# Optional expert tiles moved to the front of a routed MoE stage, behind one condition

## The chip, the core and the metric

One core of a Trainium2 chip runs the whole program. The metric is device time in microseconds; lower is better. Five engines work side by side, each with an instruction queue of its own: TensorE (PE in the profile, its weight loads PEld), VectorE (DVE), ScalarE (ACT), GpSimd (POOL) and SyncE (SP, which issues most DMAs). They meet only through semaphores. A condition at run time is evaluated by each engine that has instructions in its body: it loads a value into a register (TENSOR_LOAD), compares and branches.

## The reference

```python
x = retention(q, k, v)                 # 8 x 8 heads x 576 x 64, becomes x[4608, 512]
logits = x @ w_gate + modality_bias[modality_id]       # 8 experts
e_idx = argmax(logits); gate_w = softmax(logits)[e_idx]
for e in range(8):                     # first mixture: each token goes to one expert
    out[e_idx == e] = gate_w * (relu(x[e_idx == e] @ w1[e]) @ w2[e])
# second, soft mixture over out: 32 slots
logits = out @ phi
d = softmax(logits, over tokens); slot_input = d.T @ out
slot_out = relu(slot_input @ m1[e]) @ m2[e]            # 4 slots for each of 8 experts
y = softmax(logits, over slots) @ slot_out
```

## The kernel before

**Three stages.** First the retention over 36 chunks of 128 tokens (written to `xd`), with the gate and a routing that scatters each token's number and gate weight to its expert's place in a table `tb`. Then the expert slots. Last the soft mixture's two layers and the output (lines 614 to 690).

**The slots.** Sorted by expert, the tokens fill tiles of 128; an expert's last tile is partly empty. There are at most NSLOT = 43 tiles and at least NSURE = 36; how many there are, `tot`, is known only at run time. `slot(i)` (line 530 on) works on tile i: 24 matmuls of 512 columns (L473, numbered m = 1 to 24; the first 12 give half h=0 of the hidden layer, the others h=1), each weight split into a high part `wh` and a low part `wl`. Between them stand hooks: `at(n, f)` puts f behind matmul n. So the parts of three tiles overlap in one slot: `emit_xT` for the next tile, `emit_hT`, `emit_l2` for the one before, the softmax parts `emit_sel`, `emit_z`, `emit_G` for the one before that. `places(i+4)` (SyncE) loads a tile's rows of `tb`, `gather(i+3)` (GpSimd) fetches the tokens by them.

**Change of expert.** `if_change(k, engines, f)` runs f on the engines named if tile k belongs to another expert than tile k-1. At a change the new expert's w1, waiting in `raw[h]`, is split into `wh[h]` and `wl[h]`, in four pieces each: ScalarE copies (L106), VectorE subtracts pieces 0 and 1 (L111), GpSimd pieces 2 and 3 (L107). The hooks for this are s0 = 17 (h=0) and s1 = 24 (h=1), with VectorE's share under conditions of its own at d0 = 17 and d1 = 25, which is m = 1 of the next slot. Behind it `load_raw` loads the next expert's half, and one slot later `emit_SI` adds up what the old expert's tokens give (L518 to L527).

**Index chain.** A table R on partition 0, one row for each slot and one ahead of them (`reg(-1, ...)`), holds the row numbers and flags that the conditions and loads read (lines 357 to 391).

**Start of the slots** (from line 574): `places(0..3)`; then GpSimd gathers tiles 0 and 1, `emit_xT(0)`, and GpSimd issues the loads of the first needed w1 halves and w2; the conditions for splitting w1 anew; `early` under a condition (it isn't taken here).

**End of the slots.** Slots 0 to 35 stand in one straight line. From 36 on `more(i)` nests: if n > i, slot i and `more(i+1)`, else `drain(i-1)`, which finishes the last two tiles and multiplies the result into `siT` (L604). So there are eight copies of `drain`, one for each possible end. The weights of the stage behind are loaded into memory that comes free (`piece`, `load_XL`, `later`); in the slots from 35 on these loads carry a condition, so that only the last slot's are carried out. L631 is the first product that reads `siT`.

Of the kernel before, what the change touches and what calls it, by code (L numbers as in the profile page):

```python
# [6 lines left out]
ET=mybir.EngineType  # L7
# [16 lines left out]
def host(inp):  # L24
# [40 lines left out]
    cm[6:8,368]=np.arange(2)+6  # L65
# [14 lines left out]
P=dict(A=3,B=10,wc=13,SI=14,s0=17,s1=24,d0=17,d1=25)  # L80
def body(nc,tc,I,O):
# [8 lines left out]
    with ctx, tc.manual_schedule():  # L90
# [252 lines left out]
        t8=U("t8",[E,E]); nxt=U("nxt",[E,1]); ic=U("ic",[E,NSLOT]); b1=U("b1",[E,NSLOT]); r4x=U("r4",[E,4*NSLOT+1]); r4=r4x[:,:4*NSLOT].rearrange("p (a b) -> p a b",a=4); ef=U("ef",[128,NSLOT+1]); sb=U("sb",[128,NSLOT]); rem=T("rem",[128,NSLOT])  # L343
        R=T("R",[1,NSLOT+1,4],I32); ec=U("ec",[1,NSLOT]); same=T("same",[128,NSLOT]); es=ef[:,1:]; o_=slice(0,1); i8=it[0:E]
# [9 lines left out]
        def mm_r4():  # L354
# [17 lines left out]
            lambda: V.tensor_scalar(out=r4[:,1],in0=b1,scalar1=beg,scalar2=None,op0=ALU.mult),
            lambda: V.tensor_scalar(out=r4[:,2],in0=b1,scalar1=cnt,scalar2=None,op0=ALU.mult),
            lambda: V.tensor_scalar(out=r4[:,3],in0=b1,scalar1=nxt,scalar2=None,op0=ALU.mult),
# [15 lines left out]
            lambda: V.scalar_tensor_tensor(out=rem,in0=sb,scalar=-128.0,in1=cp[3][:,2],op0=ALU.mult,op1=ALU.add)],  # L390
# [7 lines left out]
        Gs=M1.tile([128,257],F32,name="Gs"); V.memset(Gs,0.0)  # L398
# [29 lines left out]
        for t in xg: V.memset(t,0.0)  # L428
        for t in hh: V.memset(t[:,:,256],1.0)
# [10 lines left out]
        for j in range(6):  # L440
            ring("ui",j,6,[128,1],U32,pl=P0)
# [90 lines left out]
        def slot(i,first=False):  # L532
# [6 lines left out]
            if i+1<NSLOT: at(P['wc'],lambda: emit_wc(i+1))  # L539
            if NSURE<=i+2<=NSLOT: at(P['wc'],lambda: SP.dma_start(out=XW,in_=half(NPF+3,1),cond=nsp==i+2))  # L540
# [162 lines left out]
```

## Time and profile before

| | us |
|---|---|
| median of 3 runs | 651.0 (650.69 to 653.0) |
| profiled execution | 651.03 |
| its span in the profile | 649.4 |
| TensorE busy | 598.3 |
| VectorE / ScalarE / GpSimd busy | 319.1 / 208.5 / 245.9 |
| mean granted TensorE clock | 0.967 of full speed |

The retention takes the span up to about 178 us, the slots from 188 to 559, the rest is the end. [...] In a row of the order in time the bracket at the end tells how long the engine had been idle and what ended that; "issue" means that the profile shows nothing that it waited for, and a name with q (ACTq L530) is an engine's queue at a condition of that line.

### The profile page before, as it was taken

To read this page: it belongs to the slowest core of one execution; us is meant where nothing else is said; L and a number is where in the kernel's file an instruction comes from. 1 tells how busy PE (TensorE), PEld (TensorE's weight loads), DVE (VectorE), ACT (ScalarE), POOL (GpSimd) and SP (SyncE) were. 2 spreads that over 40 slices of the span, in tenths; PEclk is the share of its full clock that TensorE was granted. 3 is DMA by queue.
4 is the path that set the end of the run, shared out by engine and by line. 5 is a ranking of instruction groups with operands and counts; after the bars stand their busy time and mean duration, and the time that the engine had idled before them with its cause. 6 is when DMAs were issued, how large, how long until landed. Compare 5 with 4: busy or idle time off the path is not lost. (4 is left out here: it accounts for less than half of the span.)

```text
span 649.4 us, 17574 instructions
## 1 busy us (share of the span) xinstructions
PE 598.3 (92%) x6122; PEld 441.1 (68%) x6122; DVE 319.1 (49%) x934; ACT 208.5 (32%) x545; POOL 245.9 (38%) x351
## 2 busy tenths in 40 slices
PE   8899999999989999988999999999998999779982
PEld 5788888888557667755677777777775777453552
DVE  2455555667616443575455444545555544322342
ACT  1222323343225232453233233233343232212242
POOL 3534445545646233374343344344355343110000
PEclk8999999999979999988999999999999999889997
DMA  8999999997958820147455554444414401849888
GB/s 301 405 369 389 415 417 395 372 340 256 360 212 301 327 85 5 38 148 280 163 167 167 167 164 140 136 147 154 167 28 158 166 11 40 313 168 360 340 290 292
DMA packets 48247, 148.58 MB, mean 229 GB/s; under 512 B 12276, under 2 KB 23935, under 8 KB 37888
## 3 DMA queue, kind: packets, MB, share of 16 engines
q1 hardware_dynamic: 41936, 132.60, 55.8%
q0 software_dynamic: 6192, 14.53, 6.5%
q8 instruction: 58, 0.95, 0.6%
q14 instruction: 61, 0.50, 0.2%
HBM read 291.93 MB, written 27.71 MB: 492 GB/s over the span
## 5 line engine op out<-in xcount | busy, mean ns | idle before, releaser
L473 PE MATMUL ps_L<-wh,xl 128*128 128x512 f32 x624 | 212.2, 411 | 0.9 <-ACTq L530 0.9
L473 PEld LDWEIGHTS ps_L<-wh,xl 128*128 128x128 f32 x624 | 116.0, 191 | 38.8 <-issue 16.9
L473 PE MATMUL ps_L<-wl,xl 128*128 128x512 f32 x312 | 126.9, 407 | 4.9
L473 PEld LDWEIGHTS ps_L<-wl,xl 128*128 128x128 f32 x312 | 59.4, 190 | 31.9 <-issue 21.9
L477 DVE TENSOR_SCALAR hh<-ps_L,gi 128x512 f32<-128x512 f32 x39 | 29.3, 751 | 97.4 <-PE ps_L L473 97.3
L182 DVE TENSOR_TENSOR st_s<-ps_s,cm 128x512 f32<-128x512 f32 x72 | 47.8, 683 | 37.4 <-PE ps_s L179 31.2
L170 POOL TENSOR_TENSOR vh<-kqv,vtab 128x512 f32<-128x512 f32 x36 | 37.3, 1036 | 65.4 <-PE ps_st L191 47.4
L495 ACT ACTIVATE z<-ps_z,mt 32x128 f32<-32x128 f32 x39 | 14.0, 360 | 148.7 <-DVE mt L494 148.7
L509 POOL TENSOR_SCALAR cy<-cx,cm 128x32 f32<-128x32 f32 x39 | 14.4, 369 | 121.0 <-DVE cm L508 116.5
L510 POOL DMA_INDIRECT cs<-cy,ui x39 | 42.2, 1082 | 16.6 <-POOL cy L509 13.3
L179 PE MATMUL ps_s<-kqv 64*128 64x128 f32 x576 | 43.1, 288 | 1.5 <-DVE st_s L182 1.4
L206 PE MATMUL ps_x<-st_s,vh 128*64 128x128 f32 x576 | 41.1, 287 | 2.2 <-POOL cum L155 2.2
L261 POOL DMA_INDIRECT tb<-gk,idx x36 | 36.0, 1000 | 17.6 <-DVE r_cn L257 5.9
L179 PEld LDWEIGHTS ps_s<-kqv 64*128 64x128 f32 x576 | 35.9, 190 | 8.5 <-issue 3.8
L482 PE MATMUL ps_h<-cs__100,hh 128*128 128x128 f32 x312 | 41.3, 276 | 0.0
L218 ACT COPY xr<-ps_t 128x512 f32<-128x512 f32 x36 | 21.1, 586 | 60.5 <-PE ps_t L217 51.8
L210 DVE TENSOR_TENSOR xT<-ps_x,gt 128x512 f32<-128x512 f32 x36 | 24.9, 691 | 27.0 <-PE ps_x L206 24.5
L206 PEld LDWEIGHTS ps_x<-st_s,vh 128*64 128x64 f32 x576 | 32.1, 141 | 8.3 <-issue 5.7
L476 ACT ACTIVATE hh<-ps_L,gi 128x512 f32<-128x512 f32 x39 | 26.9, 690 | 31.8 <-PE ps_L L473 31.8
L482 PEld LDWEIGHTS ps_h<-cs__100,hh 128*128 128x128 f32 x312 | 36.2, 143 | 0.1
L454 POOL DMA_INDIRECT xr__2950<-xd,ui x28 | 29.4, 1051 | 16.5 <-POOL ui L453 8.7
L462 DVE TENSOR_TENSOR xl<-ps_xT,xl 128x512 fp32r<-128x512 f32 x40 | 27.2, 681 | 10.6 <-ACT xl L462 10.6
(235 smaller groups left out, 961.0 us busy)
## 6 DMA issues: line engine op xcount, KB each, us to landing
raw<-in_w SPq DMA_DIRECT2D x79, 1024.0 KB
w<-in_w SPq DMA_DIRECT2D x38, 2048.0 KB
kqv<-in_qkv SPq DMA_DIRECT2D x28, 1024.0 KB
m<-in_m SPq DMA_DIRECT2D x19, 1024.0 KB
xd<-xr SPq DMA_DIRECT2D x32, 256.0 KB
wh<-mx SPq DMA_DIRECT2D x8, 1024.0 KB
wl<-mx SPq DMA_DIRECT2D x8, 1024.0 KB
w2T<-in_w2T SPq DMA_DIRECT2D x12, 512.0 KB
```

The source lines that it names most:

```text
L170: G_.tensor_tensor(out=t,in0=kqv[g][:,2].rearrange("p (h d) -> p h d",h=H),in1=bc(vtab[:,pos_(g)],[128,H,D],2),op=ALU.mult)
L179: r=slice(64*h,64*h+64); PE.matmul(out=pss[h][:,p],lhsT=pk(g,0)[r,p],rhs=pk(g,1)[r,p],start=True,stop=True)
L182: V.tensor_tensor(out=st,in0=pss[h],in1=bc(masks[g%NCH],[128,NP,128],1),op=ALU.mult)
L206: PE.matmul(out=xo(g,p,h),lhsT=v[:,2*p+h],rhs=sts[g,h][:,p],start=c in(0,4) and p<2,stop=p>1,skip_group_check=True)
L261: nodep(G_.indirect_dma_start(out=tb,out_offset=bass.IndirectOffsetOnAxis(ap=idx[:,k:k+1],axis=0),in_=gk[:,k],in_offset=None),"tb")
L454: G_.indirect_dma_start(out=xg[i%3],out_offset=None,in_=xd,in_offset=bass.IndirectOffsetOnAxis(ap=u,axis=0),bounds_check=NTOK-1,oob_is_err ...
L462: A.copy(out=hi,in_=ps); V.tensor_tensor(out=lo,in0=ps,in1=hi.bitcast(F32),op=ALU.subtract)
L473: PE.matmul(out=ps,lhsT=a[:,c],rhs=w[h][:,s],start=n==0,stop=n==11); n+=1; m+=1
L476: if h==0: A.activation(out=d,in_=q,func=AF.Relu,scale=g)
L477: else: V.tensor_scalar(out=d,in0=q,scalar1=0.0,scalar2=g,op0=ALU.max,op1=ALU.mult)
L482: for c in range(4): PE.transpose(out=ps[:,c],in_=hh[i%2][:,2*half+c//2,(c%2)*128:(c%2)*128+128],identity=ident)
L510: nodep(G_.indirect_dma_start(out=cs,out_offset=bass.IndirectOffsetOnAxis(ap=gi[i][1],axis=0),in_=y,in_offset=None,bounds_check=NTOK-1,oob ...
```

## The change

The tiles are aligned to the end: the last tile is always slot 42, and slot i is used if n > 42 - i. So with fewer than 43 tiles the first slots are the empty ones.

- Slots 0 to 3 (NRARE = 4), with `early` and their own first loads, stand in one outer condition on all five engines. It is taken only with 40 tiles or more, or when expert 6 or 7 starts early.
- Slots 4, 5 and 6 stand in one condition each; their Else does what the next slot needs (`places`, `gather`, `emit_xT`, `emit_wc`).
- Slots 7 to 42 and `drain(42)` are straight. The loads for the stage behind stand in slots 41 and 42 without a condition.
- The gathers of tiles 4 to 6 stand behind the outer condition. The first weights are loaded by SyncE instead of GpSimd.
- The split is regrouped: h=0 for all three engines under one condition at m = 13; pieces 0 and 1 of h=1 at 24; pieces 2 and 3 of h=1 at 29, that is m = 5 of the next slot.
- The index chain counts from the end: seven small instructions more on VectorE. Buffers that a skipped slot would leave unwritten are cleared: on VectorE two of 1028 columns and several small ones, on GpSimd eight small ones.
- `load_WT` for experts 6 and 7 moves one tile later, with its products (`moe_W`) at m = 16 instead of 12.

```diff
-P=dict(A=3,B=10,wc=13,SI=14,s0=17,s1=24,d0=17,d1=25)
+P=dict(A=3,B=10,wc=13,SI=14,s0=13,s1=24,s2=29)
...
-        def splita(h):
-            for c in range(4):
+        def split_(h,cs):
+            for c in cs:
                 s=slice(c*512,c*512+512)
                 A.copy(out=wh[h][:,s],in_=raw[h][:,s])
-                if c>1: G_.tensor_tensor(out=wl[h][:,s],in0=raw[h][:,s],in1=wh[h][:,s].bitcast(F32),op=ALU.subtract)
-        def splitd(h):
-            for c in range(2):
-                s=slice(c*512,c*512+512)
-                V.tensor_tensor(out=wl[h][:,s],in0=raw[h][:,s],in1=wh[h][:,s].bitcast(F32),op=ALU.subtract)
+                (V if c<2 else G_).tensor_tensor(out=wl[h][:,s],in0=raw[h][:,s],in1=wh[h][:,s].bitcast(F32),op=ALU.subtract)
...
-            lambda: V.tensor_scalar(out=ic,in0=i8,scalar1=1.0,scalar2=ee[:,E:],op0=ALU.add,op1=ALU.min),
+            lambda: V.tensor_scalar(out=ic,in0=i8,scalar1=ee[:,E:],scalar2=float(1-NSLOT),op0=ALU.add,op1=ALU.add),
+            lambda: V.tensor_scalar(out=icc,in0=ic,scalar1=1.0,scalar2=None,op0=ALU.max),
...
+            lambda: V.tensor_scalar(out=few,in0=ee[0:1,E:],scalar1=NSLOT-NRARE+0.5,scalar2=None,op0=ALU.is_lt),
+            lambda: V.tensor_scalar(out=c64,in0=cp[4],scalar1=64.0,scalar2=None,op0=ALU.add),
...
+            lambda: V.scalar_tensor_tensor(out=R[:,0,0:1],in0=few,scalar=-64.0,in1=c64,op0=ALU.mult,op1=ALU.add),
+            lambda: V.scalar_tensor_tensor(out=R[:,0,1:2],in0=same[o_,0:1],scalar=0.0,in1=few,op0=ALU.is_equal,op1=ALU.mult),
...
-        for t in xg: V.memset(t,0.0)
-        for t in hh: V.memset(t[:,:,256],1.0)
+        for t in (*xg,Gs): V.memset(t,0.0)
+        for t in hh: V.memset(t,0.0); V.memset(t[:,:,256],1.0)
...
+            G_.memset(ring("pad",j,2,Z),-1e30); G_.memset(ring("wc",j,2,[128,256]),0.0); G_.memset(ring("p",j,2,[128,32]),0.0); G_.memset(ring("mt",j,2,[128,4]),0.0)
...
-                for h in range(2):
-                    at_(P['s%d'%h],lambda k=k,h=h: if_change(k,[ET.Activation,ET.Pool],lambda: splita(h)))
-                    at_(P['d%d'%h],lambda k=k,h=h: if_change(k,[ET.DVE],lambda: splitd(h)))
-                    at_(max(P['s%d'%h],P['d%d'%h]),lambda k=k,h=h: load_raw(k,[h]))
-            if i+1>=NSURE:
-                c=dict(cond=nsp<=i+1) if i+1<NSLOT else {}
-                at(12,lambda: SP.dma_start(out=XR[:,0:1024],in_=half(15,1)[:,1024:2048],**c))
-                at(12,lambda: piece(NPF+2,**c)); at(12,lambda: load_XL((i+1)%2,**c)); at(24,lambda: piece(NPF+1,**c))
+                for n,h,cs,e in ((P['s0'],0,range(4),[ET.Activation,ET.DVE,ET.Pool]),(P['s1'],1,range(2),[ET.Activation,ET.DVE]),(P['s2'],1,range(2,4),[ET.Activation,ET.Pool])):
+                    at_(n,lambda k=k,h=h,cs=cs,e=e: if_change(k,e,lambda: split_(h,cs)))
+                    if 3 in cs: at_(n,lambda k=k,h=h: load_raw(k,[h]))
+            if i+1==NSLOT:
+                at(12,lambda: SP.dma_start(out=XR[:,0:1024],in_=half(15,1)[:,1024:2048]))
+                at(12,lambda: piece(NPF+2)); at(12,lambda: load_XL((i+1)%2)); at(24,lambda: piece(NPF+1))
...
-        for j in range(4): places(j)
-        gather(0); gather(1); emit_xT(0)
-        load_raw(-1,q=G_,eng=ET.Pool); gather(2); load_w2(0)
-        for h in range(2): if_change(0,[ET.Activation,ET.DVE],lambda: split(h))
-        load_raw(0)
+        for j in range(NRARE,NRARE+4): places(j)
...
-        with tc.If(reg(-1,2,[ET.PE,ET.Activation,ET.SP],NSLOT)>0): early()
-        emit_wc(0)
-        for i in range(NSURE):
...
+        def optional(i):
+            with tc.If(n>NSLOT-1-i) as arm: slot(i)
+            with arm.Else():
+                places(i+4); gather(i+3)
+                if i+1!=NRARE: emit_xT(i+1); emit_wc(i+1)
+        all_=[ET.PE,ET.Activation,ET.DVE,ET.Pool,ET.SP]
+        with tc.If(reg(-1,0,all_,64+NSLOT)>0):
+            with tc.If(reg(-1,2,[ET.PE,ET.Activation,ET.SP],NSLOT)>0): early()
+            with tc.If(n>NSLOT-NRARE):
+                for j in range(4): places(j)
+                gather(0); gather(1); load_raw(-1,q=G_,eng=ET.Pool); gather(2); load_w2(0)
+                for h in range(2): if_change(0,[ET.Activation,ET.DVE],lambda: split(h))
+                load_raw(0)
+                emit_xT(0); emit_wc(0)
+                for i in range(NRARE): optional(i)
+
+        gather(NRARE); gather(NRARE+1); gather(NRARE+2)
+        e=reg(-1,3,[ET.SP],8)
+        for h in range(2): SP.dma_start(out=raw[h],in_=I['w1'][e,:,h],cond=n<NSLOT-NRARE+1)
+        e=reg(0,1,[ET.SP],7); SP.dma_start(out=w2,in_=I['w2'][e],cond=n<NSLOT-NRARE+1)
+        for h in range(2):
+            with tc.If(reg(-1,1,[ET.Activation,ET.DVE],1)>0): split(h)
+        e=reg(0,3,[ET.SP],8)
+        for h in range(2): SP.dma_start(out=raw[h],in_=I['w1'][e,:,h],cond=reg(-1,1,[ET.SP],1)>0)
+        emit_xT(NRARE); busy(5); emit_wc(NRARE)
+        for i in range(NRARE,NSLOT-NSURE): optional(i)
+        for i in range(NSLOT-NSURE,NSLOT):
+            slot(i)
...
-        def more(i):
-            if i==NSLOT: return drain(i-1)
-            with tc.If(n>i) as arm:
-                slot(i); more(i+1)
-            with arm.Else(): drain(i-1)
-        more(NSURE)
+        drain(NSLOT-1)
```

## Rows read from the trace of the kernel before

**Rows 1.** Page: a whole engine, and VectorE's line that runs once a slot.

```profile
PE 598.3 (92%) x6122; PEld 441.1 (68%) x6122; DVE 319.1 (49%) x934; ACT 208.5 (32%) x545; POOL 245.9 (38%) x351
...
L477 DVE TENSOR_SCALAR hh<-ps_L,gi 128x512 f32<-128x512 f32 x39 | 29.3, 751 | 97.4 <-PE ps_L L473 97.3
```

**Rows 2.** Stretches: start:end length, busy time (instructions) by engine, TensorE clock, DMA.

```profile
275.20:288.60 13.40, 10.83 (x64) 7.16 (x63) 9.35 (x20) 7.45 (x18) 9.51 (x10) 0.87 0.52 180
288.60:304.10 15.50, 12.94 (x83) 8.06 (x82) 8.73 (x21) 5.74 (x15) 11.03 (x12) 0.89 0.54 178
...
482.20:494.40 12.20, 9.58 (x65) 6.73 (x64) 8.16 (x18) 5.60 (x14) 9.34 (x10) 1.00 0.55 197
...
550.00:558.80 8.80, 8.62 (x64) 6.27 (x62) 4.46 (x15) 2.85 (x8) 3.24 (x5) 1.00 0.67 233
558.80:563.10 4.30, 0.00 (x0) 0.00 (x0) 0.75 (x1) 0.00 (x0) 0.00 (x0) 0.92 0.99 372
563.10:568.90 5.80, 5.37 (x35) 3.43 (x35) 2.63 (x13) 1.39 (x5) 0.36 (x1) 0.50 1.02 382
568.90:580.20 11.30, 10.50 (x73) 7.92 (x73) 4.07 (x18) 1.78 (x8) 2.41 (x3) 0.83 0.31 102
580.20:583.00 2.80, 0.00 (x0) 0.00 (x0) 0.00 (x0) 0.18 (x1) 0.00 (x0) 0.99 0.82 292
583.00:588.40 5.40, 5.35 (x33) 2.52 (x33) 0.29 (x1) 0.90 (x4) 0.00 (x0) 0.69 0.91 316
588.40:638.30 49.90, 45.94 (x481) 24.20 (x480) 21.38 (x37) 19.08 (x44) 0.00 (x0) 1.00 0.88 329
```

**Rows 3.** Order in time, TensorE at the end: start, duration, what, idle before.

```profile
563.15 0.76 PE L491 MATMUL ps_z<-l,cs__100 128*128 128x128 f32 x2 [4.38 <-issue]
...
583.05 1.07 PE L631 MATMUL q_h<-wh,siT 128*32 128x512 f32 x2 [3.17 <-DMA cB<-cs]
```

**Rows 4.** The same view, ScalarE's copy of siT.

```profile
579.91 0.27 ACT L604 COPY siT<-ps_g 128x128 f32<-128x128 f32 x1 [4.04 <-PE ps_g L603]
```

**Rows 5.** The same view, all engines, in front of the first slot.

```profile
181.85 0.19 POOL L453 CAST ui<-gi 128x1 uint32<-128x1 f32 x1 [4.99 <-DMA gi<-tb]
...
184.03 0.44 PE L283 MATMUL ps_wt<-cs__100,wt 128*128 128x128 f32 x2 [0.46 <-ACT Wall L284]
...
184.51 0.37 ACT L284 COPY Wall<-ps_wt 128x256 f32<-128x256 f32 x1 [0.53 <-PE ps_wt L283]
...
186.29 0.66 PE L460 MATMUL ps_xT<-cs__100,xr__2950 128*128 128x128 f32 x4 [1.82 <-DMA xr__2950<-xd,ui]
...
187.66 0.69 DVE L462 TENSOR_TENSOR xl<-ps_xT,xl 128x512 fp32r<-128x512 f32 x1 [7.82 <-ACT xl L462]
...
187.84 1.36 PE L473 MATMUL ps_L<-wh,xl 128*128 128x512 f32 x2 [0.89 <-ACTq L530]
```

**Rows 6.** The same view, VectorE clears a buffer of 512 columns.

```profile
179.19 0.48 DVE L428 MEMSET xg<- 128x512 f32 x1
```

**Rows 7.** DMA issues: what, queue, count, size, median time to landing in us.

```profile
raw<-in_w POOLq DMA_DIRECT2D x2, 1024.0 KB, 6.4
```

**Rows 8.** Order in time at the change of expert at 482 us.

```profile
480.68 4.27 ACT L106 CAST wh<-raw 128x512 fp32r<-128x512 f32 x8 [0.57 <-ACTq L530]
...
482.43 5.95 POOL L107 TENSOR_TENSOR wl<-raw,wh 128x512 fp32r<-128x512 f32 x4 [1.55 <-ACT wh L106]
...
483.42 2.61 DVE L111 TENSOR_TENSOR wl<-raw,wh 128x512 fp32r<-128x512 f32 x2
...
487.31 0.33 PE L502 MATMUL ps_z<-cs__100,z 128*128 128x128 f32 x1 [1.21 <-DVE z L496]
...
489.23 0.63 PE L488 MATMUL ps_z<-xr__2950,wc 128*32 128x128 f32 x12 [1.18 <-DVE xr__2950 L483]
```

**Rows 9.** Order in time in an ordinary slot, ScalarE and GpSimd.

```profile
554.57 0.29 ACT L506 ACTIVATE cx<-ps_z,cm 128x32 f32<-128x32 f32 x1 [1.50 <-PE ps_z L488]
...
555.59 0.37 POOL L509 TENSOR_SCALAR cy<-cx,cm 128x32 f32<-128x32 f32 x1 [2.75 <-DVE cm L508]
```

More of the change, by code (lines that the diff above doesn't have):

```diff
@@ L18 @@
 NSLOT=43; NSURE=36
+NRARE=4
 GR=[(0,5),(5,4),(9,5),(14,4),(18,5),(23,4),(27,4),(31,3),(34,2)]
@@ L372, in body @@
[L372 to L374 removed]
+            lambda: V.tensor_scalar(out=begs,in0=beg,scalar1=float(NSLOT),scalar2=ee[:,E:],op0=ALU.add,op1=ALU.subtract),
+            lambda: V.scalar_tensor_tensor(out=b1c,in0=icc,scalar=beg,in1=r4[:,0],op0=ALU.is_gt,op1=ALU.subtract),
@@ new lines, in body @@
+            lambda: V.scalar_tensor_tensor(out=b1,in0=ic,scalar=0.0,in1=b1c,op0=ALU.is_gt,op1=ALU.mult),
+            lambda: V.scalar_tensor_tensor(out=r4x[:,4*NSLOT:],in0=begs,scalar=cm[0:E,368:369],in1=nf,op0=ALU.is_lt,op1=ALU.mult),
+            lambda: V.tensor_scalar(out=bt_,in0=begs,scalar1=cm[0:E,369:370],scalar2=None,op0=ALU.add),
+            lambda: V.scalar_tensor_tensor(out=bc_,in0=begs,scalar=128.0,in1=cnt,op0=ALU.mult,op1=ALU.add),
+            lambda: V.tensor_scalar(out=r4[:,1],in0=b1,scalar1=bt_,scalar2=None,op0=ALU.mult),
@@ L538, in slot @@
             at(1,lambda: emit_pad(i))
-            if i+1<NSLOT: at(P['wc'],lambda: emit_wc(i+1))
-            if NSURE<=i+2<=NSLOT: at(P['wc'],lambda: SP.dma_start(out=XW,in_=half(NPF+3,1),cond=nsp==i+2))
-            if 2<=i<4: at(8,lambda: load_WT(i+4,0)); at(20,lambda: load_WT(i+4,1))
-            if 4<=i<6: at(12,lambda: moe_W(i+2)); at(22,lambda: moe_WT(i+2))
+            if i+1<NSLOT and i+1!=NRARE: at(P['wc'],lambda: emit_wc(i+1))
+            if i+2==NSLOT: at(P['wc'],lambda: SP.dma_start(out=XW,in_=half(NPF+3,1)))
+            if 7<=i<9: at(8,lambda: load_WT(i-1,0)); at(20,lambda: load_WT(i-1,1))
+            if 9<=i<11: at(16,lambda: moe_W(i-3)); at(22,lambda: moe_WT(i-3))
             if i>1: at(P['A'],lambda: emit_sel(i-2)); at(P['B'],lambda: emit_z(i-2))
             if i>0: at(P['A'],lambda: emit_hT(i-1,0)); at(P['A'],lambda: emit_hT(i-1,1)); at(P['B'],lambda: emit_l2(i-1))
-            if i+1<NSLOT: at(P['A'],lambda: emit_xT(i+1))
+            if i+1<NSLOT and i+1!=NRARE: at(P['A'],lambda: emit_xT(i+1))
             if i>1:
@@ L582, in early @@
                 moe_W(e); moe_WT(e)
-        with tc.If(reg(-1,2,[ET.PE,ET.Activation,ET.SP],NSLOT)>0): early()
-        emit_wc(0)
-        nsp=nc.values_load(tot[0:1,0:1],engines=[ET.SP],min_val=0,max_val=NSLOT,skip_runtime_bounds_check_because="it is a sum of counts")
-        for i in range(NSURE):
-            slot(i)
-            x,h=divmod(i-12,2)
-            if 0<=x<NPF: piece(x,[h])
-            elif 0<=x-NPF<2 or x==NPF+2 and h==0: SP.dma_start(out=mx[x-NPF][:,2048*h:2048*h+2048],in_=half(MX[x-NPF],h))
         n=nc.values_load(tot[0:1,0:1],engines=[ET.PE,ET.Activation,ET.DVE,ET.Pool,ET.SP],min_val=0,max_val=NSLOT,skip_runtime_bounds_check_because="it is a sum of counts")
@@ L594, in busy @@
             for _ in range(n): PE.matmul(out=ring("ps_L",0,2,[128,512],pl=PX)[:,0:128],lhsT=sel,rhs=ident,start=True,stop=True)
+        def optional(i):
[25 more added lines that the diff above has]
+            slot(i)
+            x,h=divmod(i-16,2)
+            if 0<=x<NPF: piece(x,[h])
+            elif 0<=x-NPF<2 or x==NPF+2 and h==0: SP.dma_start(out=mx[x-NPF][:,2048*h:2048*h+2048],in_=half(MX[x-NPF],h))
         def drain(i):
```

29 lines of the change are left out of this document (14 added, 15 removed).

## The prediction

> **What bounds the kernel now.** I read the page first: TensorE is busy for 92% of the span [rows 1]. That share hides where TensorE stands still, so the second view was the table of stretches, cut at the ends of expert slots and at the joints between stages [rows 2]. An ordinary slot (550.0 to 558.8) takes 8.8 us and TensorE works 8.62 of them at clock 1.00: nothing off TensorE counts there. Three slots are longer, those around a change of expert: 13.4, 15.5 and 12.2 us, with VectorE and GpSimd at 8 to 11 us busy. Then comes the joint behind the last slot: 4.3 us without a single matmul, 5.8 us at clock 0.50, 11.3 at 0.83, 2.8 again without one, and 5.4 at 0.69. From 588.4 on TensorE is busy 45.94 of 49.9 us at clock 1.00, so the tail is its own bound. The third view, TensorE's order in time, names the two stops [rows 3]: before L491 (4.38, "issue": no other engine is waited for) and before L631 (3.17). ScalarE's row shows that the second stop is not for data of this chain: siT is written by 579.91 + 0.27 = 580.18 [rows 4], and the first matmul that reads it starts at 583.05. In the code both places are jumps: `more(39)` fails and all engines leap to `drain(38)` in the innermost Else, and behind `drain` they leap over the arms of the other ends. The transfer that is named for the second wait was issued in front of a jump of the same length, so I put that stop down to the jump. The last view is the joint in front of the slots [rows 5], where TensorE waits 1.82 for the first gather and 0.89 for ScalarE's conditions.
>
> 39 tiles run here (VectorE's L477 runs once a slot, x39 [rows 1]). With the change the outer condition is therefore not taken (39 < 39.5, and no expert 6 or 7 starts early), slots 4, 5 and 6 run inside one condition each, 7 to 42 straight, and `drain(42)` follows without a jump.
>
> **The end (gain).** L491 starts at 563.15 after 4.38 idle, so the last slot's products end at 558.77 [rows 3]; without the jump L491 follows them as it does inside the slots: 4.38 saved. The stretch at clock 0.50 held 5.37 us of TensorE work [rows 2]; at clock 1.00 that is 2.7, and since VectorE's copies stand between I count 2.5. Without the second jump L631 starts at siT: 583.05 - 580.18 = 2.87 [rows 3, 4]. The next stretch, 5.35 us of TensorE work at clock 0.69 [rows 2], would be 3.7 at clock 1.00: 1.65 less. Sum 11.4. What is late next: the weights for L631, loaded into wh[1] and wl[1] once the last slot has read them. The DMA engines are full until 568.9 and then at 0.31 of 11.3 us, 3.5 us of work [rows 2]: they land by about 572, 13 us behind the last slot. The shortened chain needs 21.4 - 4.38 - 2.5 = 14.5 us from 558.77 to siT (580.18 - 558.77 = 21.4), so 1.5 us are left. Because that is thin, and because TensorE has gaps in the chain in which its clock may fall again, I take 10.5 of the 11.4. Lower end 7.2, the two stops alone; upper end 11.4.
>
> **The start (cost).** All five engines meet the outer condition and jump over its body, four slots and `early`: the jump is about as long as the one at the end. No row shows such a jump here, so its price is bounded by the two at the end, 2.87 and 4.38, and from below by 0, if the target is already in the engine. The first came with DMA engines at 0.99, the second at 0.82 [rows 2]; at the start they are nearly empty, so I take the lower, 2.87. TensorE's last product of the stage before ends at 184.03 + 0.44 = 184.47, ScalarE's last copy at 184.51 + 0.37 = 184.88 [rows 5]. TensorE is back at 187.3, ScalarE at 187.75. ScalarE now has its two split conditions ahead of its half of `emit_xT` instead of behind; a condition costs it 0.57 (the idle time that L530 ends [rows 8]), so 188.9. From the transposes to the first L473 it is 187.84 - 186.29 = 1.55 us now; of that I count 0.65, ScalarE's copy, behind ScalarE's arrival: L473 at 189.5 instead of 187.84, +1.7. TensorE has idled longer by then; for a longer stretch at half clock I add 0.6: **+2.3**. Bounds: 0, and 4.38 - 2.87 = 1.5 more for the jump, 1.5 for the clock: +5.3.
> Hidden at the start: GpSimd's jump and its new memsets lie under its wait of 4.99 us for the table rows (`places` stays ahead of the condition) [rows 5]; if that cover is gone they cost some 2 us. VectorE has seven more small instructions in the index chain (0.15 each, about 1 us) and two memsets of 1028 columns (twice 0.48 for 512 each, so 2 us [rows 6]): it has 7.82 us idle there [rows 5]. Its jump fits behind them, but with nothing to spare. First weights: three loads leave GpSimd's queue, each issued there in front of a gather, and go to SyncE behind its own jump. They took 6.4 us to land [rows 7]. SyncE ends the four `places` at about 183, so it issues at 187 to 190 and the halves land at 193 to 197; they are first read at m=13 of the first slot, about 6 us behind its first product, 195.6. Hidden, or up to 2 us late.
> [...]
>
> **Slots 4 to 6.** Three conditions with an Else of some ten instructions to jump over, instead of three without. The conditions of the slots 36 to 38 cost nothing that the slots' length shows: 550.0 to 558.8 is one of them [rows 2]. The end of a body adds a short jump for each engine. Between 0 and 0.6 each; I take 0.2: +0.6.
>
> **The split of new weights (gain).** At a change ScalarE copies eight pieces in a row (480.68, 4.27 us), VectorE subtracts the last two until 483.42 + 2.61 = 486.03, and GpSimd works 5.95 [rows 8]. Behind that stand VectorE's and ScalarE's parts of the softmax, and TensorE waits 1.21 and 1.18 for them. With the change the first half begins at m=13, about 0.5 us earlier; two of ScalarE's eight copies (1 us) and GpSimd's last two subtractions move to m=5 of the next slot, behind these parts. I expect both waits to shrink to about 0.9 together: -1.5 for the change at 482. At 275 the same, and the clock 0.87 there [rows 2] recovers: -2.5. The change at 288 follows one slot later, and the second half's next load now starts behind GpSimd's later subtraction, with up to 6.4 us to land [rows 7]: it is late by about as much as is won, 0. Sum -4.0; I take **-3.5**, bounds -6.5 (all three waits gone) and +2 (the late load costs more).
>
> **Ordinary slots.** ScalarE gets a third condition, at m=5; it waits 1.50 us before cx there, more than the 0.57. GpSimd waits 2.75 before cy [rows 9]. Both stay covered: 0. The memory loads of slots 35 to 38 that were issued under a condition and skipped go away; SyncE bounds nothing there.
>
> **Rivals.** (1) The end is held by transfers: wh[1] and wl[1], or cs, which TensorE needs one block of L631 later, land late. For: 1.5 us of slack. Against: SyncE no longer stalls in its own jump. TensorE would stand 3.17 as now and fall back in clock, 1.65: 4.8 given back, 644.7. (2) The stop only moves to the front: all engines pay 4.38, the clock stays low and the first weights are late by 2, so 7.3 instead of 2.3: 645. (3) The long jump is free, because its target is already in the engines: 637.6. [...] (4) **Slower:** the third condition of each slot lies on the path. Then 36 slots pay 0.4 each, 14.4, less the 11.1 won: 654. It decides from the point where ScalarE's conditions take more than the 1.50 us in front of cx [rows 9]; the row speaks against it. (5) The change doesn't do what it says: the outer condition is taken after all, and the inner one (n > 39) fails and makes the same leap one condition later, 0.57 dearer: 640.5.
>
> **How the numbers follow.** -10.5 + 2.3 + 0.6 - 3.5 = -11.1. The profiled execution took 651.03 us (span 649.4), the median is 651.0: 639.9, so 640. Its own range is 635 to 645. Chances: forecast 0.53, (1) 0.14, (2) 0.10, (3) 0.10, (4) 0.11, (5) 0.02. A measurement of this kernel can tell about 0.5% from no change, 3.3 us: faster is below 647.7. (1) and (2) reach past that with about a quarter of their chance. Low end: 11.4 + 6.5 won and nothing lost is 633; 634 leaves out little. High end 650: it leaves out (4) and little else. Of the forecast's own chance 0.05 leaks past 647.7. Faster 0.78, same 0.10, slower 0.12.
>
> **What would show it.** In the table of stretches: no stretch without matmuls behind the last slot, clock near 1.00 there, siT 14 to 16 us behind the last L473, and L631 right behind siT. At the start a stop of TensorE of 3 to 5 us between the last L283 and the first L473, where 3.4 stand now. Slots after a change of 10 to 12 us instead of 12.2 and 13.4, ordinary ones of 8.8. The prediction is wrong if ordinary slots grow, if the stop at the front is over 8 us, or if L631 waits for wh.

## The result and the profile after

The changed kernel takes 660.2 us (median of four executions, 658.3 to 662.5) against 651.4 us beside it: ratio 1.013, 95% interval 1.009 to 1.017. The forecast was 640. The profiled execution took 662.5 us, its span is 660.9 us (before 649.4), the mean clock 0.967 in both.

The table of stretches of the kernel after, cut as before: the joint in front of the slots, the first four used slots, the two slots at 300 us where the expert changes twice in a row, an ordinary slot, the end, the first products behind siT. Columns as in [rows 2].

```profile
185.50:202.30 16.80, 2.83 (x14) 2.86 (x15) 0.69 (x1) 1.27 (x3) 4.71 (x7) 0.56 0.77 293
202.30:212.30 10.00, 9.85 (x65) 7.39 (x64) 4.98 (x16) 4.95 (x12) 2.62 (x5) 0.89 0.10 29
212.30:227.20 14.90, 11.94 (x65) 9.19 (x64) 6.56 (x17) 5.25 (x13) 8.68 (x9) 0.77 0.43 140
227.20:240.20 13.00, 11.20 (x83) 7.16 (x81) 5.37 (x18) 3.41 (x10) 3.61 (x6) 1.00 0.28 76
240.20:250.00 9.80, 8.97 (x65) 6.73 (x64) 4.43 (x15) 2.85 (x8) 3.24 (x4) 1.00 0.82 312
299.60:310.30 10.70, 9.53 (x65) 6.68 (x64) 7.49 (x19) 7.05 (x17) 8.80 (x10) 1.00 0.49 149
310.30:327.10 16.80, 12.91 (x83) 8.15 (x82) 6.63 (x21) 5.88 (x15) 9.30 (x11) 0.90 0.66 215
555.20:564.00 8.80, 8.65 (x64) 6.64 (x64) 4.44 (x15) 2.85 (x8) 2.12 (x3) 1.00 0.02 5
581.10:595.50 14.40, 12.07 (x112) 8.03 (x111) 7.27 (x31) 3.22 (x13) 3.81 (x5) 1.00 0.84 325
595.50:602.00 6.50, 5.73 (x52) 1.67 (x52) 1.18 (x3) 1.02 (x5) 0.00 (x0) 1.00 0.75 236
```

Three things are read from it. The end did what was forecast: 14.4 us at clock 1.00 between the last slot and the first product behind siT, where 24.2 us with two stops stood (558.8 to 583.0, [rows 2]). An ordinary slot still takes 8.8. And 16.8 us lie between TensorE's last product of the stage before and the first L481 (L473 before), with TensorE busy for 2.83 of them; before it was 184.47 to 187.84, 3.37 us [rows 5]. The four slots behind are 10.0, 14.9, 13.0 and 9.8 us long.

The balance against the kernel before, by the same ends: L281 (before L283) ends 1.0 later, the joint is 13.5 longer, the first four slots cost 10.0 more (where the expert first changes, 212.3 to 227.2 at clock 0.77, most), the slots up to the last give back 2.2, the end 10.8. 1.0 + 13.5 + 10.0 - 2.2 - 10.8 = 11.5, the growth of the span.

**The joint**, in order of time: SyncE's queue, GpSimd, TensorE.

```profile
184.56 0.19 POOL L461 CAST ui<-gi 128x1 uint32<-128x1 f32 x1 [6.65 <-SPq L595]
185.05 0.44 PE L281 MATMUL ps_wt<-cs__100,wt 128*128 128x128 f32 x2 [0.46 <-ACT Wall L282]
187.00 1.47 SPq L607 DMA_DIRECT2D raw<-in_w  x2
189.58 0.34 SPq L608 DMA_DIRECT2D w<-in_w  x1
190.38 1.08 POOL L462 DMA_INDIRECT xr__2961<-xd,ui  x1 [5.63 <-PEq L595]
...
199.47 1.09 PE L468 MATMUL ps_xT<-cs__100,xr__2961 128*128 128x128 f32 x4 [13.99 <-DMA xr__2961<-xd,ui]
200.35 2.34 PE L588 MATMUL ps_L<-cs__100 128*128 128x128 f32 x10
202.34 1.20 PE L481 MATMUL ps_L<-wh,xl 128*128 128x512 f32 x2
```

What the outer condition (L595) issues, by engine, from the view of that line; the three numbers are the shortest, median and longest ns. Below it, who waited for it, in us and times.

```profile
L595 SPq EVENT_SEMAPHORE  x9: 17/17/17, 184.1 to 184.7; - x9
...
L595 POOLq INC_SWDGE_SEM  x1: 896/896/896, 180.5 to 180.5; - x1
...
L595 PEldq COMPARE_BRANCH  x1: 3374/3374/3374, 186.1 to 186.1; - x1
L595 ACTq COMPARE_BRANCH  x1: 50/50/50, 186.4 to 186.4; - x1
...
  POOL ui L461: 6.7, 1
  POOL xr__2961 L462: 5.6, 1
```

Behind its branch each engine that skips the body still has semaphore steps of the condition's line (SyncE nine, 184.1 to 184.7); I read them as a catch-up to the counts that the body would have left. GpSimd waited for this catch-up twice (6.65 and 5.63 us). Its first step (ui) waits for SyncE's, until 184.56 instead of 181.85 [rows 5]. Its gather waits for TensorE's, since the skipped slots read the buffer that it writes, and TensorE hangs 3.37 us in its branch. Meanwhile SyncE has issued 4 MB of first weights, and the gather lands behind them. The row of the kernel before shows the gather at 183.04, 3.25 us ahead of the transposes at 186.29:

```profile
183.04 1.07 POOL L454 DMA_INDIRECT xr__2950<-xd,ui  x1 [1.00 <-DMA gi<-tb]
```

After, it is 9.09 (190.38 to 199.47). So the gather is issued 7.3 later and takes 5.8 longer to land, less the 1.0 by which L281 is late: 12.2. The other 1.3 are the five filling products in front of L481 (L588) and a lower clock.

### The profile page after: what moved, and what is told of

It reads as the page before. It is cut to its first block, busy times and chain, and to the rows that moved or that the text cites. A ratio compares the mean times of both kernels' runs of the same rounds, so it can differ in the third digit from the quotient of the medians.

```text
span 660.9 us, 17737 instructions
## 1 busy us (share of the span) xinstructions
PE 598.3 (91%) x6174; PEld 441.4 (67%) x6174; DVE 321.3 (49%) x973; ACT 210.0 (32%) x552; POOL 243.5 (37%) x354
## 5 line engine op out<-in xcount | busy, mean ns | idle before, releaser
L481 PE MATMUL ps_L<-wh,xl 128*128 128x512 f32 x624 | 212.1, 409 | 4.2 <-DVE wl L109 1.6
L481 PEld LDWEIGHTS ps_L<-wh,xl 128*128 128x128 f32 x624 | 115.3, 190 | 43.1 <-issue 17.3
L481 PE MATMUL ps_L<-wl,xl 128*128 128x512 f32 x312 | 126.7, 406 | 5.2
L481 PEld LDWEIGHTS ps_L<-wl,xl 128*128 128x128 f32 x312 | 59.3, 190 | 32.5 <-issue 22.7
L518 POOL DMA_INDIRECT cs<-cy,ui x41 | 44.2, 1077 | 17.1 <-POOL cy L517 14.1
L490 PE MATMUL ps_h<-cs__100,hh 128*128 128x128 f32 x320 | 42.7, 277 | 0.2 <-DVE hh L485 0.2
L462 POOL DMA_INDIRECT xr__2961<-xd,ui x26 | 27.6, 1061 | 30.3 <-PE ps_xT L468 7.6
```

Source lines behind the costliest of these rows:

```text
L462: G_.indirect_dma_start(out=xg[i%3],out_offset=None,in_=xd,in_offset=bass.IndirectOffsetOnAxis(ap=u,axis=0),bounds_check=NTOK-1,oob_is_err ...
L481: PE.matmul(out=ps,lhsT=a[:,c],rhs=w[h][:,s],start=n==0,stop=n==11); n+=1; m+=1
L490: for c in range(4): PE.transpose(out=ps[:,c],in_=hh[i%2][:,2*half+c//2,(c%2)*128:(c%2)*128+128],identity=ident)
L518: nodep(G_.indirect_dma_start(out=cs,out_offset=bass.IndirectOffsetOnAxis(ap=gi[i][1],axis=0),in_=y,in_offset=None,bounds_check=NTOK-1,oob ...
```

## The experiments

Each run is compared with runs of the kernel before on the same chip, where that took 649 to 651 us (the pair above, and a0 with x5 to x7) or 656. "Joint" is the time from the end of the last L281 to the first product of the first slot. A diff is against the changed kernel unless it says otherwise.

| run | ratio to before (95%) | joint, us |
|---|---|---|
| changed kernel, three chips | 1.013, 1.015, 1.019 | 16.9, 17.2, 17.4 |
| x1 gathers ahead | 1.011 (1.006 to 1.015) | 9.2 |
| x2 weights behind | 1.011 (1.007 to 1.016) | 11.5 |
| x3 both | 1.023 (1.018 to 1.028) | 18.9 |
| x4 short body | 0.999 (0.996 to 1.002) | 3.2 |
| f4 body of two slots | 1.015 (1.010 to 1.020) | 10.8 |
| x5 slots 4 to 6 straight | 1.010 (1.005 to 1.016) | 16.9 |
| x7 no parts for empty tiles | 1.012 (1.006 to 1.018) | 16.5 |
| x6 old split | 1.016 (1.011 to 1.022) | 17.2 |
| e1 before, end straight | 0.983 (0.977 to 0.989) | 2.2 |
| f2 e1 and new split | 0.989 (0.983 to 0.994) | 2.2 |
| x8 x4, x5 and x7 | 0.990 (0.987 to 0.993) | 4.0 |
| f1 x8, old loads and split | 0.985 (0.980 to 0.991) | 3.9 |
| c1 mended | 0.997 (0.995 to 0.999) | 7.8 |
| c2 39 tiles as a path | 0.996 (0.992 to 0.999) | 9.7 |
| f3 two conditions | 0.997 (0.994 to 1.001) | 8.1 |
| c4 two hops | 0.999 (0.996 to 1.002) | 8.9 |

**The changed kernel again**, as the measure on other chips: a0 beside x5 to x7, a1 beside c4.

> The changed kernel as it is, once more, as the measure for what runs beside it on this chip: 1.013 times the kernel before, 13.5 us or more between the end of the last L281 and the first L481.

> The changed kernel as it is, beside the version with two short jumps on the same chip: 1.013 to 1.020 times the kernel before, 16.5 to 17.5 us between the end of the last L281 and the first L481.

It lost 1.5% and 1.9%, with the same joint. One stretch differs between these executions of one and the same kernel, and it bears on every comparison below: the slot where the expert first changes took 14.8 in a0 (14.9 in the first profile, at clock 0.77) and 12.1 in a1, at clock 1.00.

```profile
218.50:230.60 12.10, 9.14 (x65) 6.72 (x64) 6.47 (x17) 5.03 (x12) 8.62 (x9) 1.00 0.46 137
```

The groups of x1 to x4, of e1 and of f1 to f4 met a kernel before of 656 us, as a1 did; a1's 1.019 is the nearest measure for them.

**x1: the gathers ahead of the condition.**

```diff
+        gather(NRARE); gather(NRARE+1); gather(NRARE+2)
         with tc.If(reg(-1,0,all_,64+NSLOT)>0):
...
-        gather(NRARE); gather(NRARE+1); gather(NRARE+2)
```

> The changed kernel with one move: the gathers of tiles 4 to 6 stand ahead of the outer condition again. Theory (the first gather is late: it waits behind the skipped body for the other engines, and then lands behind 4 MB of weights): the gather issues at about 183 as in the kernel before and lands at 186.3; TensorE comes back from its jump at 189.5, the first L481 starts at 192.4 instead of 202.3: ten us less, about 650. Rival A (the long jump itself is the price): the jump is unchanged, so at most 1 us is won, 659. Rival B (the rest, from the first slot's end on, is what counts: conditions of the slots and the new split): the first product is earlier, but the slots behind it lose the same, 657 or more.

The joint is 7.7 to 8.2 shorter. What holds TensorE now is its own branch, and behind it GpSimd's catch-up. The condition's line, then TensorE in order of time:

```profile
L596 PEldq COMPARE_BRANCH  x1: 4294/4294/4294, 192.9 to 192.9; - x1
```

```profile
198.59 1.09 PE L468 MATMUL ps_xT<-cs__100,xr__2961 128*128 128x128 f32 x4 [6.30 <-DMA xr__2961<-xd,ui]
```

The gather was issued at 189.55, ahead of everything; the transposes start 1.4 us behind the end of TensorE's branch. So the gather's place was worth 8 us of the joint, and rival A (at most 1 us) falls, but the jump is still there. The time fell by less than the theory's ten: by the ratios 5 us against a1. The slots took 379.2 us from first product to last, where a1's took 376.2, at the change of expert above all (14.9 against 12.1, at clock 0.77 against 1.00), so rival B isn't needed for the rest.

**x2: the first weights on GpSimd, behind two gathers.**

```diff
-        gather(NRARE); gather(NRARE+1); gather(NRARE+2)
+        gather(NRARE); gather(NRARE+1); load_raw(-1,q=G_,eng=ET.Pool); gather(NRARE+2); load_w2(0)
-        for h in range(2): SP.dma_start(out=raw[h],...)    (and the load of w2)
```

> The changed kernel with one move: the first weights are issued by GpSimd behind two gathers, as in the kernel before, not by SyncE; the gathers stay behind the outer condition. Theory: the gather still issues at 190.4, but lands in about 3.3 us instead of 9.0, so the first L481 is 5.8 us earlier, 196.5, and the time about 654.5. If the weights don't stand in its way, nothing changes: 660.

```profile
196.62 1.08 POOL L462 DMA_INDIRECT xr__2961<-xd,ui  x1 [8.19 <-PEq L595]
...
200.05 1.09 PE L468 MATMUL ps_xT<-cs__100,xr__2961 128*128 128x128 f32 x4 [8.62 <-DMA xr__2961<-xd,ui]
```

The gather lands in 3.4 us (196.62 to 200.05) instead of 9.1, and the joint is 5.9 shorter than in a1: as the theory has it. By the ratios the time fell by 4.9.

**x3: both, the old order on GpSimd, all of it ahead of the condition.**

```diff
+        gather(NRARE); gather(NRARE+1); load_raw(-1,q=G_,eng=ET.Pool); gather(NRARE+2); load_w2(0)
         with tc.If(reg(-1,0,all_,64+NSLOT)>0):
...
-        gather(NRARE); gather(NRARE+1); gather(NRARE+2)    (and the loads behind it)
```

> The changed kernel with the whole order of the kernel before at the front: two gathers, the w1 halves, a gather and w2, all on GpSimd and all ahead of the outer condition. Theory: the two parts of the loss don't add here, since TensorE's return at 189.5 ends both: first L481 at 192.4, about 650, the same as with the gathers alone moved. Rival A (jump): 659. If weights on SyncE also hurt the second gather, this one is 1 to 2 us better than the gathers alone.

It is the worst of all; both theories fail. GpSimd in order of time, and its part of the condition:

```profile
194.16 0.55 POOL L430 DMA_DIRECT2D w<-in_w  x1
207.80 0.18 POOL L461 CAST ui<-gi 128x1 uint32<-128x1 f32 x1 [13.09 <-DMA raw<-in_w]
```

```profile
L596 PEldq COMPARE_BRANCH  x1: 5854/5854/5854, 192.1 to 192.1; - x1
...
L596 POOLq INC_SWDGE_SEM  x1: 1032/1032/1032, 206.5 to 206.5; - x1
```

GpSimd's step that brings its DMA semaphores up (INC_SWDGE_SEM) comes here only when its transfers in flight have landed, the 4 MB at 206.4 (in x1, with gathers alone in flight, at 197.5). TensorE waits for it too (16.03 us, until 207.58). So 4 MB in flight on GpSimd's queue at this condition made the joint 18.9 us, where x1, with gathers alone, has 9.2.

**x4 and f4: the length of the skipped body.** The body without its four optional slots, and with two of them; it is not entered.

```diff
-                for i in range(NRARE): optional(i)
+                for i in range(2): optional(i)        (f4; x4 has none)
...
```

> The changed kernel with the four optional slots left out of the outer condition's body, which is never entered here: what is computed stays the same, the jump is a quarter as long. Theory: TensorE's 3.4 us stop at its branch goes, the gather that waits for it issues 2 to 3 us earlier, and the first L481 comes at about 199.5: 657. Rival A (the long jump is the price): most of the 14.5 us go, 647. If the stop doesn't depend on the length of the jump: 660.

> The changed kernel with two optional slots in the outer body instead of four (it is never entered). The jump's price on TensorE was 0.37 us without a slot, 3.4 to 4.3 with four, 7.0 with seven. If it grows with what is skipped: 1.7 to 2.2. If it is paid once the target lies too far: 0.4 or 3.4.

TensorE's branch in x4, then in f4 with who waits for it:

```profile
L595 PEldq COMPARE_BRANCH  x1: 373/373/373, 191.7 to 191.7; - x1
```

```profile
L595 PEldq COMPARE_BRANCH  x1: 367/367/367, 193.6 to 193.6; - x1
...
  POOL xr__2961 L462: 4.8, 1
```

x4 went as rival A said, 3.2 us of joint. But leaving the slots out takes two things away: the long branch, and the slots' reads of the gather's buffer, for which the gather had to wait. f4 keeps the second: its branch is as short (0.37), and the joint is still 10.8. So of the 14 us 6.6 hang on the long branch (17.4 in a1 to 10.8) and 7.6 on what waits behind it (10.8 to 3.2). Of the 6.6 the branch itself is 3.4 (3.79 in a1); the rest is the landing: the weights now start only 0.4 us ahead of the gather (194.59 and 195.00), which lands in 6.0 us instead of 9.1. f4's time shows less than its joint, because its first two slots took 24.3 us where a1's took 21.2, at clock 0.88 instead of 1.00 in the second.

**x5: slots 4 to 6 without their conditions.** `optional(i)` becomes `slot(i)` for i = 4 to 6.

> The changed kernel with slots 4, 5 and 6 in one straight line instead of one condition each (right for these data, which have 39 tiles). Theory: at the end of a conditional slot TensorE waits for the other engines' last steps in it (1.24 for ScalarE's and 1.57 for VectorE's split at the first change, 0.67 and 0.68 for VectorE's queue at the two other ends) and, at the first, falls back in clock; without the conditions slot 5 takes about 11.5 instead of 14.9, slot 6 12.1 instead of 13.0, slot 7 8.8 instead of 9.7: 5 us less than the changed kernel. Rival (the earlier start of the new split, and not the conditions, makes these waits): less than 1 us.

TensorE's order at the ends of these slots in the changed kernel, then the stretches of x5 (slots 5, 6 and 7):

```profile
213.59 0.50 PE L481 MATMUL ps_L<-wh,xl 128*128 128x512 f32 x1 [1.24 <-ACT wh L108]
215.66 0.80 PE L481 MATMUL ps_L<-wh,xl 128*128 128x512 f32 x1 [1.57 <-DVE wl L109]
...
228.12 0.50 PE L481 MATMUL ps_L<-wh,xl 128*128 128x512 f32 x1 [0.67 <-DVEq L538]
```

```profile
210.80:221.50 10.70, 9.51 (x64) 6.69 (x64) 6.31 (x17) 5.03 (x12) 8.63 (x9) 1.00 0.51 142
221.50:233.60 12.10, 10.97 (x82) 7.24 (x82) 5.38 (x19) 3.41 (x10) 4.96 (x8) 1.00 0.44 133
233.60:242.30 8.70, 8.55 (x64) 6.58 (x63) 4.42 (x15) 2.85 (x8) 1.88 (x3) 1.00 0.86 345
```

10.7, 12.1 and 8.8 instead of 14.8, 13.0 and 9.7 in a0: 6.0 us. All these stops are gone, and the 0.68 at the end of slot 6 too. 2.7 of the 6.0 is the clock at the first change: against a1's 12.1, 13.0 and 9.7, at clock 1.00 as here, it is 3.3. By the medians it is 3.5 (657.5 against 661.1). The rival (less than 1) falls, and the theory's 5 is met only where the clock fell.

**x7: no parts for the two empty tiles** that stand ahead of the first used one.

```diff
-            if i>1: at(P['A'],lambda: emit_sel(i-2)); at(P['B'],lambda: emit_z(i-2))
+            if i>1 and i-2 not in (2,3): at(P['A'],lambda: emit_sel(i-2)); at(P['B'],lambda: emit_z(i-2))
```

and the same for emit_G, and for emit_hT and emit_l2 of tile 3.

> The changed kernel without the parts of slots 4 and 5 that work for the two tiles ahead of the first used one (their softmax parts, their second layer, their share of G, their rows of cs; those tiles are empty here, so nothing of the result is left out). Theory: TensorE has 40 short products less in slot 4 and 18 less in slot 5, at half clock: 1 to 2 us less than the changed kernel. If these parts hide behind other waits: 0.

```profile
200.70:208.10 7.40, 7.25 (x30) 5.34 (x29) 1.98 (x3) 3.65 (x7) 1.09 (x3) 0.88 0.13 37
208.10:221.20 13.10, 10.08 (x54) 7.46 (x53) 4.46 (x6) 4.52 (x9) 7.49 (x8) 0.87 0.47 148
```

The first two used slots take 7.4 and 13.0 instead of 9.9 and 14.8 in a0: 4.2 us by these two traces, where 1 to 2 were expected. The counts show what is gone: 30 products in the first slot instead of 65. How much time it is stays open: the second slot ran at clock 0.87 here and at 0.77 in a0, a1 took 9.1 and 12.1 with all the parts in, and by the medians it is 2.9 with executions that overlap (656.8 to 660.2 against 659.3 to 662.9).

**x6 and f2: the split.** x6 has the old hooks (s0 = 17, s1 = 24, d0 = 17, d1 = 25); f2 is the kernel before with a straight end and the new hooks.

> The changed kernel with the old order of the split (both halves for ScalarE and GpSimd at m = 17 and 24, VectorE's under conditions of its own). Theory: the five changes of expert behind lose about 1.5 us together (slot 9 +2.8, slot 31 +1.2, the slots behind them -2.5), the first one hardly changes. Rival: the first change's stops of 1.24 and 1.57 come from the new order; then it is 3 us less there and 1.5 less in all.

> The kernel before with two parts of the change: the straight end and the new split (right for 39 tiles). Theory: the split wins about 3 us at the first of two changes in a row and gives most of it back in the next slot, where ScalarE waits 3 us for the later load of w1; 1 to 1.5 us in all, ratio 0.981 against 0.983 with the straight end alone. By the prediction's 3.5 us it would be 0.978; if the late load costs more than is won, 0.985.

x6's median is that of a0 (661.4 and 661.1). In its trace the change at 299 us takes 13.6 instead of 10.7, the slot behind it 15.4 instead of 16.8. The first change takes 12.1 instead of 14.8, but a1 took 12.1 there with the new split, at clock 1.00 like x6: that difference is the clock's, and neither the theory's 1.5 us nor the rival's is shown. f2 is 0.006 above e1, 3.7 us, and above all three of its expectations, though the intervals overlap: the new split wins nothing there either. Its first change takes 13.3 where e1's takes 8.2. Why, in f2 at the first change, and in the changed kernel at the double one:

```profile
208.89 0.50 PE L469 MATMUL ps_L<-wl,xl 128*128 128x512 f32 x1 [3.81 <-POOL wl L107]
```

```profile
313.43 1.14 ACT L108 CAST wh<-raw 128x512 fp32r<-128x512 f32 x2 [2.83 <-DMA raw<-in_w]
```

GpSimd's last two subtractions now stand behind a gather that waits for its table rows; and the next expert's second half is loaded later, so that ScalarE waits 2.8 for it in the slot after.

**e1: the end alone**, on the kernel before.

```diff
-        more(NSURE)
+        for i in range(NSURE,39): slot(i)
+        drain(38)
```

> The kernel before with its end alone made straight: slots 36 to 38 and the last two tiles' rest follow without conditions (right for these data, 39 tiles). Theory: this is the part of the change that works; without both stops and at the full clock the end is 10.8 us shorter, ratio 0.983 to the kernel before. If the gain came from the loads that the change moved, or if the next stage's weights come late, less than 7 us: 0.99.

0.983, 11.2 us of 655.9: the forecast's first term, by itself.

**x8 and f1: everything undone.** x8 is x4, x5 and x7 in one; f1 adds x2's order of the loads and the old split, without the filling products.

> The changed kernel with all three suspects gone at once (right for these data): the optional slots left out of the outer condition's body, slots 4 to 6 straight, no parts for the two empty tiles. Theory: the three add up to the whole loss: front 17.2 to 3.3 us, slots 6.0, empty tiles 4.2, so 24 us less than the changed kernel and 12 to 13 less than the kernel before: ratio 0.980. If something else of the change costs as well, the ratio stays above 0.988.

> The changed kernel with the four optional slots left out of the outer body, slots 4 to 6 straight, no parts for the two empty tiles, and now also the first weights behind two gathers on GpSimd, the five filling products away, and the old split. Theory: with the order of the first loads and the split of the kernel before, nothing of the loss is left: ratio 0.983 to 0.985, as with the straight end alone. Rival (the longer index chain, or slots counted from the end, cost by themselves): 0.988 or more.

x8 stays 0.010 above its expectation: in its first slot TensorE waits for the second gather, which is still behind the weights, and its double change took 29.7 us where e1's took 28.1 (both of one trace each).

```profile
197.81 0.90 PE L468 MATMUL ps_xT<-cs__100,xg 128*128 128x128 f32 x4 [2.04 <-DMA xg<-xd,ui]
```

f1 comes to 0.985, e1's 0.983 within the intervals. What is left of the change (the index chain, slots counted from the end) costs 1.5 us by the two ratios, which is inside the noise (each interval is almost 4 us either way).

**c1, c2, f3, c4: versions for any number of tiles.** All have gathers ahead of the condition (two, c4 one), no filling products, and the parts for tiles 2 and 3 in the outer body. c1 has the old split; c2 puts 39 tiles into an Else of their own with slots 4 to 6 straight; f3 keeps the body of four slots and has one condition for slots 4 to 6:

```diff
-        for i in range(NRARE,NSLOT-NSURE): optional(i)
+        with tc.If(n>NSLOT-1-NRARE) as arm:
+            for i in range(NRARE,NSLOT-NSURE): slot(i)
...
```

c4 is f3 with the old split, the body cut into two conditions of two slots each, all but one gather behind them, and the first weights on GpSimd between the gathers.

> A version for any number of tiles: two gathers ahead of the outer condition and one behind it, the five filling products away, the parts for tiles 2 and 3 in the body of the outer condition, the old split. Theory: the front is held by TensorE's jump alone, 0.6 + 3.4 to 4.3, then 2.5 to the first product: 7.5 us instead of 17.2; 4.2 less for the empty tiles; the conditions of slots 4 to 6 stay: 14 us less than the changed kernel, ratio to the kernel before 0.996. If the GpSimd queue still has to wait for its gathers to land before TensorE can go on, 3 us more: 1.000.

> The version above with the new split, and with the common number of tiles, 39, as a path of its own: the outer condition's body holds everything for other numbers, its Else slots 4 to 6 in one line. Theory: the conditions' 6 us go down to one end of a condition (0.7), so about 5 us better than the version above: ratio 0.989. If the longer jump costs TensorE in proportion to its length (seven slots instead of four), 3 us are lost again: 0.993.

> For any number of tiles: two gathers ahead of the outer condition, the parts for tiles 2 and 3 in its body, the new split, and slots 4 to 6 in one line inside one condition (39 tiles or more), whose Else holds the single ones. Theory: TensorE's jump 3.5 us in front, one end of a condition 0.7 us and a jump over two slots behind slot 6: about 2 us better than with 39 tiles as a path of their own: ratio 0.992. If the jump over the Else costs as the front one did: 0.997.

> For any number of tiles: the outer condition's body cut into two of two slots each, both behind the same condition, so that TensorE makes two short jumps instead of a long one; one gather ahead of them, the other gathers and the first weights on GpSimd behind; slots 4 to 6 in one line inside one condition; the parts for tiles 2 and 3 in the second body; the old split. Theory: each jump takes TensorE 0.4 us as with two slots, the first L481 comes about 5 us after the last L281 instead of 8 to 10, the rest as with all causes undone but for one end of a condition (1 us): ratio 0.990. If the two catch-ups of GpSimd (1 us each and the gather's landing) hold TensorE, 2 us more: 0.993. If two jumps cost what the long one did: 0.996.

TensorE's branches in c2 (one, over seven slots), then in c4 (two, over two slots each):

```profile
L607 PEldq COMPARE_BRANCH  x1: 7014/7014/7014, 192.2 to 192.2; - x1
```

```profile
L601 PEldq COMPARE_BRANCH  x1: 367/367/367, 189.6 to 189.6; - x1
...
L610 PEldq COMPARE_BRANCH  x1: 4717/4717/4717, 190.7 to 190.7; - x1
```

c1 met its number, with a joint of 7.8; in its second slot, at clock 0.76, TensorE then waits 3.0 for ScalarE's split, which itself waited 0.9 for late weights. c2 has the lowest ratio of the versions for any number of tiles, 0.4% below the kernel before, though the intervals of c1, c2 and f3 overlap; it missed both 0.989 and 0.993. Its branch took 7.0, which ate what the straight slots won (4 MB were under way meanwhile, as in x3; what made it so long isn't shown). f3's joint is 1.6 shorter than c2's, and its slots take the same 371 us, yet its ratio is no better: in its trace the end is 3.0 longer (82.5 against 79.4), because TensorE waits 1.93 for rows of cs behind the first block of products, 0.44 in c2, and the clock falls to 0.81 behind it. In c4 the second short jump costs as much as one long one, its third expectation (0.996), and with 0.999 it came out no better than that. None comes near e1, which is right for 39 tiles alone.

## Why the prediction was wrong

**The end: right.** 10.8 against 10.5, and in the way described: no stops, clock 1.00, siT 14.35 us behind the last slot's end at 581.08 (forecast 14.5), and the weights of L651 not late:

```profile
580.68 0.40 PE L481 MATMUL ps_L<-wl,xl 128*128 128x512 f32 x1
...
595.16 0.27 ACT L629 COPY siT<-ps_g 128x128 f32<-128x128 f32 x1 [4.04 <-PE ps_g L628]
...
595.48 0.62 PE L651 MATMUL q_h<-wh,siT 128*32 128x512 f32 x2 [0.35 <-ACT siT L629]
...
599.12 0.90 ACT L665 CAST chl<-xr__2961 128x128 fp32r<-128x128 f32 x4 [3.49 <-DMA xr__2961<-cs]
...
599.88 0.45 PE L668 MATMUL q_c<-identr,chl 128*96 128x128 f32 x4 [0.77 <-ACT chl L665]
```

Rival (1) falls for the weights but holds in small for cs, which it also named: one block behind siT TensorE waits 0.77 for it, so that of the 1.65 expected of the next stretch 0.9 came. In other traces with the straight end this wait is 0.4 to 2.9 us (c2, f1). Rival (5) falls: the condition was skipped.

**The start: the step that failed**, +2.3 forecast with bounds 0 to 5.3, +13.5 measured. TensorE's jump was near (2.87 taken, 3.37 measured), in part by luck: the branch behind which the 2.87 was seen took 3.93, and queued work hid the rest of it. Wrong was the paragraph "Hidden at the start". It took GpSimd's wait for the table rows as cover, and did not ask who waits behind a condition for the engines that have yet to pass it: SyncE's catch-up (2.7) and TensorE's (5.6 of waiting) came ahead of the gather. It asked of the first weights when they are read, not what they overtake: they are not late, they make the gather late by 5.8. The five filling products in the diff it did not cost at all. Rival (2) named the right place, with half the price. Rival (3), a free jump, holds for ScalarE, VectorE, GpSimd and SyncE (0.45 to 0.9 us to the next step), not for TensorE; that a target is already in an engine, its reason and that of the lower bound of 0, no run shows.

**VectorE's seven instructions** were counted under its 7.82 us of idle time. Six of them stand in front of the product that makes the table, where TensorE waits 1.51 now and 0.47 before; L281 ends 1.0 later.

```profile
176.99 0.53 PE L353 MATMUL ps_c<-r,cm 8*128 8x173 f32 x2 [1.51 <-DVE r L378]
```

**Slots 4 to 6: +0.6 forecast, 3.3 to 6.0 measured (3.5 by the medians).** The step went by slots 36 to 38 of the kernel before, whose conditions show nothing. But those are nested and close behind `drain`; where a slot's condition closes before the next one begins, TensorE waited for the other engines' last steps (1.24, 1.57 and 0.67 us in the changed kernel; gone in x5). The range is the clock, which fell to 0.77 at the first change in some executions and not in others. And the two empty tiles' parts, 2.9 us by the medians and 4.2 by the traces (x7), were in no term: the pipeline of three tiles runs on over tiles that were skipped.

**The split: -3.5 forecast.** The waits did shrink (10.7 instead of 13.4 at the first of the two changes in a row), but the next slot gives back 1.3, more than the 0 that was taken, and the first change of all, which had no term, grows with the new split in the kernel before (8.2 in e1, 13.3 in f2). The five slots around the later changes won 1.4 together; over the whole kernel it wins nothing that shows (x6) or costs 3.7, with overlapping intervals (f2).

**Ordinary slots: 0, right.** Rival (4), the forecast's slow case, falls; the loss came from the front, of which rival (2) had half, and from the first four slots, which no rival had.

## What to carry to other kernels

A condition on all engines was a meeting here: behind it GpSimd waited 6.65 us for SyncE to pass it and 5.63 for TensorE, and in x3 its own step in it stood until 206.4, when its transfers in flight had landed. So list for each queue the first instruction behind the condition, whom it waits for there, and what is issued ahead of it by others; a transfer that is on time for its reader can still make another one late (the gather took 9.09 us to land behind the weights, 3.25 before). Where work is moved into a pipeline's rare path, look at what the pipeline's later stages still do for the tiles that were left out.

## What the runs showed of the hardware

TensorE's branch took 0.37 us with no slot in the body (x4) or two (f4), and with four 3.37 (the changed kernel), 3.43 (c1), 3.79 (a1) and 4.29 (x1). It took 5.85 with four in x3, where 4 MB were under way, and 7.01 with seven in c2, where they were as well. The two stops at the end of the kernel before are such branches too (L607), 6.72 and 3.93 us long, in part hidden by queued work. Inside the branch of the changed kernel and inside each of these two starts one 16 KB packet of the queue that the profile lists as q8. From the window of the branch in the changed kernel (packets, MB, share of the DMA engines):

```profile
q8 instruction: 1, 0.02, 2.0%
```

The packet starts 1.0 us into this branch, 1.3 into the one of 3.93 and 4.35 into the one of 6.72, where the DMA engines were busy for 0.98 of the time until then (0.32 in the one of 3.93). Each of the three branches ends 1.3 to 1.4 us behind the packet's end. Packets of this queue stand elsewhere too, 58 in all in the kernel before. Whether a branch waits for such a packet is not shown, nor that the 7.01 of c2 come from seven slots of length: in x3 and c2 other transfers were under way. ScalarE took 0.45 us from the same branch to its next step in the changed kernel, but 3.5 in c1, whose body is longer. Two branches over two slots each, in a row, took 0.37 and 4.72 (c4): the second one was not cheap although it was short.
